# Retention and a squared-ReLU feed-forward on one core: two groups of retention products for each chunk instead of three

## The chip, the core and the metric

The kernel runs on one core of a Trainium2 chip. A core has a matrix engine (TensorE, "PE" in the profile; its weight loads are listed as "PEld"), a vector engine (VectorE, "DVE"), a scalar engine (ScalarE, "ACT"), a general engine (GpSimd, "POOL") and a queue that issues the transfers (SyncE, "SP"). Each engine works through its own list of instructions, and engines wait for each other only where one needs what another has made. The metric is the time of the program on the device, in microseconds (us).

## The reference

Two blocks stand one behind the other. The first is retention, an attention with a fixed decay in place of a softmax, for 8 batches of 8 heads, 576 positions and head size 64. The second is a feed-forward over all 4608 tokens, 512 to 2048 to 512, with a squared ReLU between.

```python
scores = scale * np.matmul(q, k.transpose(0, 1, 3, 2))
Dmat = np.where(rel >= 0, gamma[:, None, None] ** rel[None, :, :], 0.0)
ret = scores * Dmat[None, :, :, :]
attn_out = np.matmul(ret, v)
x = attn_out.transpose(0, 2, 1, 3).reshape(B * S, H * D)
h = np.maximum(x @ w_in, 0.0)
out = h * h @ w_out
```

`rel` is the distance between query and key, `gamma` differs by head. Since the decay is a power of the distance, it can be split into a factor for the query and one for the key, and what lies far back can be kept as one running 64x64 matrix per head.

## The kernel before

**Retention.** Each batch of 576 positions is cut into chunks of 128; the fifth chunk of a batch has only 64. There are 40 chunks, 8 of them short. A chunk is worked on in halves of 64 positions, and a head has size 64, so nearly all retention products are 64x64 products in a quarter of the TensorE array. For each chunk there are five pieces of TensorE work:

- `turn(i)` transposes k and q of the chunk (L364) into `t_ps`. ScalarE copies k to SBUF (`kT`, L370), and VectorE copies q out and multiplies it by the decay of the query (`qT`, L372). Both read the same banks, so the second waits for the first.
- `scores(i)` multiplies kT and qT of the same half (L385) into `sc_ps`, which takes the same PSUM buffer as `t_ps`. VectorE masks the result (`ret`, L388), and GpSimd multiplies v by the decay of the key (L390).
- `retain_a(i)` is the second half: scores times v within the half (L402) into `x_ps`, and the products of k and v of the first half (L405), which are added to the running matrix `u_ps`. ScalarE then copies the running matrix to SBUF (`u_sb`, L411).
- `retain_b(i)` is "q'U": the turned q times the running matrix, for both halves (L437), added into `x_ps`.
- `retain_c(i)` is the first half: scores times v (L402) and the running matrix again (L405), then its copy (L411), and the chunk's finished columns are copied from `x_ps` into `xT` (L463), where the feed-forward reads them.

The matmuls are float32; in the profile most of them stand as two records each, the transposes as one.

**A copy that orders things.** q'U and the first half add into the same columns of `x_ps`, from different rows of the array. Where other work lies between them, they are far enough apart. Where nothing lies between (the first four chunks and the last two), L447 makes a small copy on ScalarE: it reads one column of `x_ps` for each pair of heads, after q'U, and writes to a place in `u_sb` that is filled anew later. The first half waits for this copy.

**Feed-forward.** Tokens are taken in 9 blocks of 512. From the second block on, the first product (x times w_in) is not made directly: a 2x2 scheme with 7 products in place of 8 is used (`PRODUCTS`), so a block has 4 groups of 7 steps. One step, `ffn_in`, is four 128x128 by 128x256 products (eight records, L559), and each leaves work for VectorE (sums and squares, L566 to L586) or ScalarE and GpSimd (L569, L575, L576). The first block uses direct products (`first_in`, L525, 16 steps), while the weights are converted from 64-bit to 32-bit floats on VectorE and ScalarE: `convert(n)` runs the next n parts of that (L202 to L218). The second weights are converted in parts of a later list, one part behind each step. The results of the first product go to DRAM. When all retention is done, what remains of the first product follows, and then the second product runs as a stage of its own (`inner`, L748), again with 7 products, in two levels.

**The order.** The order on every engine is that of the program text: it is written out by hand in the loop of L647. Each pass mixes the retention of two neighbouring chunks with steps of the feed-forward. `ffn(i)` (L629) sets how many steps: it adds `cs / 3 * rate` to what is owed and takes steps until less than one is owed. The rate differs by stretch of tokens (L633 to L638). `retain_c` forces further steps at a block's end, so that buffers of `xT` come free (L459). Behind the fifth pass, a pass consists of three groups of retention products, with a call of `ffn` behind each: second half; q'U and scores of the next chunk; the chunk after that turned, and first half.

Of the kernel before, what the change touches and what calls it, by code (L numbers as in the profile page):

```python
# [16 lines left out]
CH = C // 2  # L17
# [23 lines left out]
def kernel(  # L41
# [33 lines left out]
    nc = tc.nc  # L75
# [16 lines left out]
    N_CH = len(chunks)  # L92
# [34 lines left out]
    def load(i):  # L127
        b, ci, c0, cs = chunks[i]
        got = {}
        for name, src, pool in (("k", k, ld4), ("q", q, ld3), ("v", v, ld4)):  # L130
            t = got[name] = pool.tile([128, H, D], F32, tag=name, name=f"{name}_ld")
            at = src[b, :, c0:c0 + cs, :].rearrange("h s d -> s h d")
            if name == "v":
                nc.sync.dma_start(t[:cs], at)
            else:

                nc.sync.dma_start(t[:cs, 0:H // 2, :], at[:, 0:H // 2, :])
                for e in range(2):
                    nc.sync.dma_start(t[:cs, H // 2 + e::2, :], at[:, H // 2 + 1 - e::2, :])
            if i < NCH and name == "q":  # L140
                nc.sync.dma_start(dq[:, :, c0:c0 + cs], decay_q[:, :, c0:c0 + cs])
        if i == 0:
            nc.sync.dma_start(dv, decay_v)
        loaded[i] = [got["q"], got["k"], got["v"]]
# [155 lines left out]
    def convert(count):  # L300
        for _ in range(count):
            f = next(w_in_steps, None)
            f and f()
# [20 lines left out]
    u_sb = [only.tile([128, HP, D], F32, name=f"u_sb{j}") for j in range(3)]  # L324
# [3 lines left out]
    N_EARLY = TOK // C  # L328
# [12 lines left out]
    def rows(half, n=64):  # L341
        return slice(64 * half, 64 * half + n)
# [4 lines left out]
    xp = [None]  # L347
    clean = set()

    def clears(half, bank):  # L350

        new = (half, bank) not in clean
        clean.add((half, bank))
        return new

    def turn(i):

        cs, c0 = chunks[i][3], chunks[i][2]
        n_h = cs // CH
        p = ps_t.tile([128, 2, 512], F32, tag="t", name="t_ps").rearrange("p h (j d t) -> p h j d t", j=2, d=HP)  # L360
        for j in (1, 0):
            for hp in range(HP):
                for h in range(n_h):
                    nc.tensor.transpose(p[:, h, j, hp, :], loaded[i][j][rows(h), 2 * hp:2 * hp + 2, :],  # L364
                                        ident[rows(h), rows(h)])
        for j, name in ((1, "kT"), (0, "qT")):
            t = st[i][name] = work2.tile([128, HP, C], F32, tag=name, name=name) if j == 0 else work.tile([128, HP, C], F32, tag=name, name=name)
            to = t[:, :, :cs].rearrange("p d (h t) -> p h d t", h=n_h)
            if j:
                nc.scalar.copy(to, p[:, :n_h, j, :, :])  # L370
            else:
                nc.vector.tensor_tensor(to, p[:, :n_h, j, :, :], dq[:, :, c0:c0 + cs].rearrange("p d (h t) -> p h d t", h=n_h),  # L372
                                        op=ALU.mult)
# [22 lines left out]
    def within(i, h):  # L396

        s = st[i]
        b_, ci, c0, cs = chunks[i]
        own, grow = [], []  # L400
        for hp, e, b in HEADS:
            own.append(lambda hp=hp, e=e, b=b: nc.tensor.matmul(  # L402
                x_at(hp, b, h), lhsT=s["vs"][rows(h), 2 * hp + b, :], rhs=s["ret"][rows(h), e, hp, :],
                start=clears(b, hp // 2), stop=False, skip_group_check=True))
            grow.append(lambda hp=hp, e=e, b=b: nc.tensor.matmul(  # L405
                u_ps[0][rows(e), hp, :], lhsT=loaded[i][1][rows(1 - h), 2 * hp + e, :], rhs=s["vs"][rows(1 - h), 2 * hp + b, :],
                start=(ci == 0 and h == 1 and hp == 0), stop=(hp == HP - 1), skip_group_check=True))
        return own, grow

    def grown(i, h):  # L410
        nc.scalar.copy(u_sb[(2 * chunks[i][1] + h + 1) % 3], u_ps[0])  # L411

    def retain_a(i):

        b_, ci, c0, cs = chunks[i]
        xp[0] = ps_x.tile([128, 2, 256], F32, tag="x", name="x_ps", padded_shape=[128, 2, 512])
        clean.clear()
        if ci == 0:
            u_ps[0] = ps_u.tile([128, HP, D], F32, tag="u", name="u_ps")
        if cs < C:  # L420
            return
        own, grow = within(i, 1)
        for j in range(0, len(own), 2):
            for f in own[j:j + 2] + grow[j:j + 2]:
                f()
        grown(i, 0)

    def retain_b(i):

        s = st[i]  # L430
        b_, ci, c0, cs = chunks[i]
        for h in reversed(range(cs // CH)):
            if 2 * ci + h == 0:
                continue
            u = u_sb[(2 * ci + h) % 3]
            for hp, e, b in HEADS[0:2] + HEADS[4:6] + HEADS[2:4] + HEADS[6:8]:
                nc.tensor.matmul(x_at(hp, b, h), lhsT=u[rows(e), hp, :], rhs=s["qT"][rows(e), hp, CH * h:CH * h + CH],  # L437
                                 start=clears(b, hp // 2), stop=False, skip_group_check=True)

    def retain_c(i):  # L440

        b_, ci, c0, cs = chunks[i]
        own, grow = within(i, 0)
        more = ci + 1 < NCH
        if i < N_EARLY or i >= N_CH - 2:

            nc.scalar.copy(u_sb[(2 * ci + (cs // CH)) % 3][:, 0:2, 0:1], xp[0][:, :, cs - CH:cs - CH + 1])  # L447
        for j in range(0, len(own), 2):
            for f in own[j:j + 2] + (grow[j:j + 2] if more else []):
                f()  # L450
        if more:
            grown(i, 1)
        tok = b_ * S + c0
        at = tok
        p = xp[0][:, :, 0:256].rearrange("p a (g t) -> p a g t", g=2)
        while at < tok + cs:
            n = at // TOK

            while steps and steps[0][0] <= (n - 2 if n > 4 else n - 3):  # L459
                step()  # L460
                owed[0] -= 1
            end = min(tok + cs, (n + 1) * TOK)
            nc.scalar.copy(xT[n][:, :, at - n * TOK:end - n * TOK].rearrange("p (a g) t -> p a g t", a=2),  # L463
                           p[:, :, :, at - tok:end - tok])
            at = end
            if n_next[0] < N_BLK and (n_next[0] + 1) * TOK <= at:
                steps.extend(block_steps(n_next[0]))
                n_next[0] += 1
        st[i] = loaded[i] = None
# [139 lines left out]
    owed = [0.0]  # L609
# [3 lines left out]
    def block_steps(n):  # L613
        if n == 0:
            return [(0, first_in, j) for j in range(N_W1)]
        return [(n, ffn_in, n, mp, j) for mp in range(N_MP) for j in range(NP)]

    def step():
        n, f, *args = steps.pop(0)
        f(*args)  # L620
# [8 lines left out]
    def ffn(i):  # L629

        b, ci, c0, cs = chunks[max(0, min(i, N_CH - 1))]
        tok = b * S + c0
        if tok < TOK + R_0:  # L633
            rate = (N_W1 - 2) / R_0 if tok >= TOK else 0
        elif tok < 5 * TOK:
            rate = (3 * N_MP * NP - LAG) / (4 * TOK - TOK - R_0 + TOK)
        else:
            rate = N_MP * NP / TOK  # L638
        owed[0] += cs / 3 * rate
        while steps and owed[0] >= 1:  # L640
            owed[0] -= 1
            if steps[0][0] == 0:
                convert(4)
            step()

    turn(0)
    for i in range(N_CH + 1):  # L647
        if i <= N_EARLY:

            if i >= 1:  # L650
                retain_a(i - 1)
                retain_b(i - 1)
                convert(2 if i >= 2 else 0)
                retain_c(i - 1)
            scores(i)
            convert(1 if i >= 2 else 0)
            if i == N_EARLY:
                step()
            turn(i + 1)
            convert((0, 2, 2, 2, 3)[i])  # L660
            if i == N_EARLY:
                step()
        else:
            retain_a(i - 1)
            convert(1)
            ffn(i - 1)
            retain_b(i - 1)
            if i < N_CH:
                scores(i)
            convert(1)  # L670
            ffn(i - 1)
            if i + 1 < N_CH:
                turn(i + 1)
            retain_c(i - 1)
            convert(1)
            ffn(i - 1)
        if i + 3 < N_CH:
            load(i + 3)
        if i < N_EARLY:
            fetch_raw(1 if i < 2 else 2)  # L680
# [183 lines left out]
```

## Time and profile before

| | |
|---|---|
| time, median of 3 runs | 1021.84 us (1021.08 to 1021.9) |
| span of the profiled execution | 1016.3 us |
| TensorE busy | 978.9 us (96%) |
| VectorE busy | 750.3 us (74%) |
| ScalarE busy | 184.6 us (18%) |
| mean of a record: step of the feed-forward (L559), retention product (L402) | 384 ns, 234 ns |

The stages, from the busy time of the engines in stretches of the span:

| us from the start | what runs | TensorE busy | VectorE busy | ScalarE busy | DMA share |
|---|---|---|---|---|---|
| 0 to 43.5 | first chunks, no feed-forward | 24.55 | 13.22 | 14.17 | 0.87 |
| 43.5 to 127 | retention and first block | 78.89 | 69.62 | 35.35 | 0.73 |
| 127 to 320 | retention and steps of 7 products | 192.72 | 149.12 | 41.00 | 0.67 |
| 320 to 556 | the same, with the second weights | 230.44 | 193.63 | 55.32 | 0.70 |
| 556 to 634 | the rest of the first product | 74.95 | 54.90 | 6.92 | 0.92 |
| 634 to 1016 | second product | 377.36 | 269.77 | 31.82 | 0.50 |

A line of the timeline has the start, the time up to the end of the last record, engine, line, operation, what is written and read, the size of the array that is used (128*128 or a part), the shape, and the number of records; in brackets stands how long the engine sat idle before, and for whom. Records of TensorE overlap, so the time from one start to the next says what work costs, not the length of one record. A line of the waits has who waited for whom, the total, how often, and the longest.

### The profile page before, as it was taken

The page shows a single profiled execution, that of the slowest core. Times are in us where ns is not written, and L with a number is a line of the kernel's source. Part 1 is how long each engine was busy: PE and PEld are TensorE (multiplying, and loading weights), DVE is VectorE, ACT ScalarE, POOL GpSimd, SP SyncE. Part 2 cuts the span into 40 slices and gives each one's busy share as a digit, 9 for nine tenths or more (in the row PEclk, how much of TensorE's full clock was granted, in tenths as well). Part 3 has the DMA queues.
Part 4 walks back from the last instruction along what each step waited for, and adds up shares of the span by engine and source line. Part 5 has one row for each costly group of instructions (what it writes and reads, how often), then busy time and mean ns, then how long its engine had stood idle before and what let it go on. Part 6 is the DMA issues. An engine that isn't in the chain of part 4 may idle for free.

```text
span 1016.3 us, 23980 instructions
## 1 busy us (share of the span) xinstructions
PE 978.9 (96%) x10376; PEld 860.9 (85%) x10376; DVE 750.3 (74%) x1398; ACT 184.6 (18%) x425; POOL 80.5 (8%) x82
## 2 busy tenths in 40 slices
PE   4799999999999999999899998999999999999998
PEld 3555488888888788888788888999999999999997
DVE  1489888657788797888976776767677676767765
ACT  2345321111213212222221010000000000000000
POOL 1110011101101112010110010000000000000000
PEclk9999999999999999999999999999999999999999
DMA  8877777647677769579446998473653636455351
GB/s 189 228 183 229 188 229 192 183 115 208 197 226 245 204 232 293 173 249 272 153 167 251 360 413 331 193 265 140 244 191 143 249 129 245 165 210 210 122 208 42
DMA packets 180232, 215.08 MB, mean 212 GB/s; under 512 B 118432, under 2 KB 128672, under 8 KB 171168
## 3 DMA queue, kind: packets, MB, share of 16 engines
q1 hardware_dynamic: 180128, 213.57, 63.8%
q8 instruction: 81, 1.33, 0.5%
q14 instruction: 23, 0.19, 0.1%
HBM read 125.19 MB, written 88.34 MB: 210 GB/s over the span
## 4 chain that ended last, share of the span: by engine, by line
PE 89%; DVE 5%; DMA 3%; ACT 1%; SPq 1%; issue 1%; DVEq 0%; ACTq 0%
PE o_b L748 16%; PE h_b L559 16%; PE o_c L748 11%; PE o_a L748 11%; PE h_a L559 10%; PE h_c L559 10%; PE h_ps L525 6%; PE x_ps L402 4%; PE t_ps L364 2%; PE x_ps L437 2%; PE sc_ps L385 2%; DMA a<-g_dram 1%; DMA w<-in_moe_w_in_dram 1%; DVE room L566 1%; PE u_ps L405 1%
## 5 line engine op out<-in xcount | busy, mean ns | idle before, releaser
L559 PE MATMUL h_b<-room,w 128*128 128x256 f32 x736 | 177.5, 384 | 1.2 <-DVE room L578 1.2
L559 PEld LDWEIGHTS h_b<-room,w 128*128 128x128 f32 x736 | 136.9, 190 | 21.1 <-DVE room L578 1.6
L748 PE MATMUL o_b<-w,room 128*128 128x128 f32 x1168 | 144.5, 275 | 0.2 <-DVE room L720 0.2
L748 PEld LDWEIGHTS o_b<-w,room 128*128 128x128 f32 x1168 | 137.2, 192 | 0.5 <-DVE room L720 0.4
L748 PE MATMUL o_c<-w,room 128*128 128x128 f32 x1008 | 123.0, 275 | 0.0
L748 PEld LDWEIGHTS o_c<-w,room 128*128 128x128 f32 x1008 | 117.7, 192 | 0.0
L559 PE MATMUL h_c<-room,w 128*128 128x256 f32 x480 | 115.8, 384 | 0.0
L559 PE MATMUL h_a<-room,w 128*128 128x256 f32 x448 | 107.5, 383 | 0.0
L559 PEld LDWEIGHTS h_c<-room,w 128*128 128x128 f32 x480 | 89.3, 190 | 12.8
L559 PEld LDWEIGHTS h_a<-room,w 128*128 128x128 f32 x448 | 83.8, 190 | 12.3 <-issue 0.5
L748 PE MATMUL o_a<-w,a 128*128 128x128 f32 x688 | 85.9, 275 | 2.8 <-DMA a<-g_dram 2.8
L748 PEld LDWEIGHTS o_a<-w,a 128*128 128x128 f32 x688 | 81.3, 192 | 3.0 <-issue 3.0
L566 DVE SCALAR_TENSOR_TENSOR room<-room 128x512 f32<-128x512 f32 x96 | 71.0, 739 | 3.3
L576 POOL TENSOR_TENSOR room<-room 128x512 f32<-128x512 f32 x32 | 35.9, 1122 | 433.6 <-ACT room L575 394.4
L759 ACT COPY r<-o_a 128x128 f32<-128x128 f32 x54 | 14.3, 265 | 276.9 <-PE o_a L748 236.2
L402 PEld LDWEIGHTS x_ps<-ret,v_ld 64*64 64x64 f32 x1152 | 42.4, 143 | 23.4 <-issue 13.9
L402 PE MATMUL x_ps<-ret,v_ld 64*64 64x64 f32 x1152 | 52.6, 234 | 9.2 <-ACT u_sb L447 5.3
L525 PE MATMUL h_ps<-room,w 128*128 128x512 f32 x128 | 59.7, 610 | 0.2 <-ACT room L463 0.2
L578 DVE TENSOR_TENSOR room<-h_b,room 128x512 f32<-128x512 f32 x32 | 22.1, 690 | 42.9 <-PE h_b L559 42.9
L372 DVE TENSOR_TENSOR qT<-t_ps,dq 128x512 f32<-128x512 f32 (+1 forms) x40 | 25.4, 634 | 36.1 <-ACT kT L370 25.8
L390 POOL TENSOR_TENSOR v_ld<-v_ld,dv 128x512 f32<-128x512 f32 (+1 forms) x40 | 44.4, 1110 | 95.5 <-DMA v_ld<-in_v_dram 74.4
L755 DVE TENSOR_TENSOR small<-o_b,small 128x128 f32<-128x128 f32 x63 | 18.4, 291 | 40.2 <-PE o_b L748 40.2
(92 smaller groups left out, 1355.5 us busy)
## 6 DMA issues: line engine op xcount, KB each, us to landing
g_dram<-room SPq DMA_DIRECT2D x36, 1792.0 KB, 7.4
a<-g_dram SPq DMA_DIRECT2D x43, 1024.0 KB, 6.3
room<-g_dram SPq DMA_DIRECT2D x20, 1024.0 KB, 6.0
w<-w_dram SPq DMA_DIRECT2D x7, 1792.0 KB, 12.3
out_dram<-room SPq DMA_DIRECT2D x18, 512.0 KB, 3.3
v_ld<-in_v_dram SPq DMA_DIRECT2D x32, 256.0 KB, 4.0
w<-in_moe_w_in_dram SPq DMA_DIRECT2D x16, 512.0 KB, 5.1
w<-in_moe_w_out_dram SPq DMA_DIRECT2D x16, 512.0 KB, 3.9
```

The source lines that it names most:

```text
L364: nc.tensor.transpose(p[:, h, j, hp, :], loaded[i][j][rows(h), 2 * hp:2 * hp + 2, :], ident[rows(h), rows(h)])
L372: nc.vector.tensor_tensor(to, p[:, :n_h, j, :, :], dq[:, :, c0:c0 + cs].rearrange("p d (h t) -> p h d t", h=n_h), op=ALU.mult)
L385: nc.tensor.matmul(sc[rows(h), e, hp, :], lhsT=kT[rows(e), hp, t], rhs=qT[rows(e), hp, t], start=True, stop=True, skip_group_check=True)
L390: nc.gpsimd.tensor_tensor(vs[:cs], vs[:cs], dv[:cs, :, ci:ci + 1].to_broadcast([cs, H, D]), op=ALU.mult)
L402: own.append(lambda hp=hp, e=e, b=b: nc.tensor.matmul(x_at(hp, b, h), lhsT=s["vs"][rows(h), 2 * hp + b, :], rhs=s["ret"][rows(h), e, hp, : ...
L437: nc.tensor.matmul(x_at(hp, b, h), lhsT=u[rows(e), hp, :], rhs=s["qT"][rows(e), hp, CH * h:CH * h + CH], start=clears(b, hp // 2), stop=Fa ...
L525: nc.tensor.matmul(p.rearrange("p h t -> p (h t)"), lhsT=w[:, c, :], rhs=xT[0][:, c, :], start=(c == 0), stop=(c == N_DM - 1))
L559: nc.tensor.matmul(p[:, mm, :], lhsT=w[:, c, :], rhs=xs[n][right][:, c, :], start=(j in OPENS and mm == 0 and c == 0), stop=(j in CLOSES a ...
L566: nc.vector.scalar_tensor_tensor(t, t, 0.0, t, op0=ALU.max, op1=ALU.mult)
L576: nc.gpsimd.tensor_tensor(g["A11"], g["A11"], g["A11"], op=ALU.mult)
L578: nc.vector.tensor_tensor(g["A22"], p, p15, op=ALU.add)
L748: nc.tensor.matmul(p, lhsT=s["lefts"][left][:, m, :], rhs=w_out[j][:, m, WO_SLOT[right], :], start=(i in OPENS and m == 0), stop=(i in CLO ...
```

## The change

The pass behind the fifth is written anew. The next chunk is turned directly behind the second half, one pass later than before, and the first half follows scores directly. So two groups remain: second half and the next chunk turned; q'U, scores and first half. Each is followed by one call of `ffn`, which now adds half of a chunk's share instead of a third. Since q'U and the first half have moved together, the ordering copy is made for every chunk, directly behind q'U. The aim is fewer changes of TensorE between small and full products.

```diff
@@ retain_b / retain_c
+        nc.scalar.copy(u_sb[(2 * ci + (cs // CH)) % 3][:, 0:2, 0:1], xp[0][:, :, cs - CH:cs - CH + 1])
+
     def retain_c(i):
...
-        if i < N_EARLY or i >= N_CH - 2:
-
-            nc.scalar.copy(u_sb[(2 * ci + (cs // CH)) % 3][:, 0:2, 0:1], xp[0][:, :, cs - CH:cs - CH + 1])
@@ ffn
-        owed[0] += cs / 3 * rate
+        owed[0] += cs / 2 * rate
@@ the loop
-            turn(i + 1)
+            if i < N_EARLY:
+                turn(i + 1)
             convert((0, 2, 2, 2, 3)[i])
...
         else:
             retain_a(i - 1)
-            convert(1)
+            if i < N_CH:
+                turn(i)
+            convert(2)
             ffn(i - 1)
             retain_b(i - 1)
             if i < N_CH:
                 scores(i)
-            convert(1)
-            ffn(i - 1)
-            if i + 1 < N_CH:
-                turn(i + 1)
             retain_c(i - 1)
             convert(1)
             ffn(i - 1)
```

## The prediction

> **What bounds the kernel now.** I read the share of busy time first, then the stages, then TensorE's timeline over one chunk, and last its waits up to 560 us, where the retention ends.
>
> ```profile
> PE 978.9 (96%) x10376; PEld 860.9 (85%) x10376; DVE 750.3 (74%) x1398; ACT 184.6 (18%) x425; POOL 80.5 (8%) x82
> ...
> PE 89%; DVE 5%; DMA 3%; ACT 1%; SPq 1%; issue 1%; DVEq 0%; ACTq 0%
> ```
>
> TensorE is busy 96% of the span and makes up 89% of the chain that ended last. In 127 to 320 us, inside the stage that changes, it is busy 192.72 of 193 us while VectorE has 149.12 and ScalarE 41.00. So in this stage the time is the sum of TensorE's issue slots, and only what shortens that sum, or a wait in it, counts. One chunk in that stretch:
>
> ```profile
> 279.56 1.99 PE L559 MATMUL h_b<-room,w 128*128 128x256 f32 x8
> 281.39 1.89 PE L559 MATMUL h_a<-room,w 128*128 128x256 f32 x8
> 283.21 0.69 PE L437 MATMUL x_ps<-qT,u_sb 64*64 64x64 f32 x32
> 283.73 0.65 PE L385 MATMUL sc_ps<-qT,kT 64*64 64x64 f32 x32
> 284.30 1.99 PE L559 MATMUL h_b<-room,w 128*128 128x256 f32 x8
> 286.13 1.89 PE L559 MATMUL h_c<-room,w 128*128 128x256 f32 x8
> 287.86 1.89 PE L559 MATMUL h_a<-room,w 128*128 128x256 f32 x8
> 289.68 0.46 PE L364 MATMUL t_ps<-ident,k_ld 64*128 64x64 f32 x8
> ```
>
> The first column is the start. Between two feed-forward steps a step takes 1.73 us (286.13 to 287.86). The step after a retention group takes 1.83 (284.30 to 286.13), the one before a group 1.82. So each entry and exit costs a tenth of a microsecond outside the group. From 279.56 to 284.30 is 4.74 us; less two steps of 1.728 the group of q'U and scores, 64 records, costs 1.284. The same sum where q'U has 16 records instead of 32 (262.40 to 268.64, three steps) gives 1.056, so a record costs (1.284 - 1.056) / 16 = 0.014, and 64 of them 0.91: the group has a fixed cost of **0.37 us**. The second half alone (273.56 to 279.56, three steps, 32 records) costs 0.816, again 0.36 above its records. Now the waits before the retention's products:
>
> ```profile
> PE x_ps L437 <- ACT u_sb L411: 5.9, 8, 2.3
> ...
> PE x_ps L402 <- ACT u_sb L447: 5.3, 5, 1.7
> PE t_ps L364 <- DVE ret L388: 4.9, 7, 0.9
> ...
> PE sc_ps L385 <- DVE qT L372: 2.0, 1, 2.0
> PE x_ps L402 <- ACT w L463: 1.6, 2, 1.1
> ```
>
> The columns are total, times, longest. The line to keep in mind is the second: it is the copy that the change now makes for every chunk, and today five of its six copies make TensorE wait.
>
> **What the Trainium skill says.** "TensorEngine Tiling (Array Packing)", Key Properties: changing the tiling mode drains TensorE, changing the tile does not. The trace agrees with 0.36 us for a visit, and with q'U and scores sharing one fixed cost. "PSUM — Partial Sum Buffer", PSUM bank collisions: two engines may not touch one bank and quadrant at once, and different row tiles must not write one bank together. That is why the copy of L447 is there: q'U and the first half reach the same bank from different rows. It is also why q's eviction (L372) comes after k's (L370): 25.8 us of VectorE's idle time end on it. "TensorE: Matmul & The Clock Gate", Architectural detail: ScalarE's queue is strictly first in, first out. So the copy waits for all that was queued ahead:
>
> ```profile
> 22.79 1.13 PE L437 MATMUL x_ps<-qT,u_sb 64*64 64x64 f32 x32 [2.30 <-ACT u_sb L411]
> ...
> 23.85 0.72 ACT L204 ACTIVATE w<-w,exp_bias 128x512 uint32<-128x512 uint32 x1 [1.11 <-DVE w L202]
> 24.48 0.64 ACT L209 ACTIVATE w<-w 128x512 f32<-128x512 uint32 x1
> 25.02 0.14 ACT L447 COPY u_sb<-x_ps 128x2 f32<-128x2 f32 x1
> ...
> 25.21 0.37 PE L402 MATMUL x_ps<-ret,v_ld 64*64 64x64 f32 x2 [1.29 <-ACT u_sb L447]
> ```
>
> The products end at 23.92, the copy takes 0.14, but it stands behind two weight conversions.
>
> **The change, part by part.** *Fewer visits.* I followed the loops with the rates of ffn and counted runs of retention work between feed-forward steps: 100 before, 69 after, since some calls of ffn give no step. That is 31 visits less. The upper price is 0.36, as q'U and scores show. The lower is the entry and exit alone, 0.10 + 0.09 = 0.19: turned chunk plus first half lasts 1.27 from its first start to the next step, and this is what the parts take singly (0.64 for a turned chunk at 47.71 us, 0.63 for a half), so a change between those two shapes eats the rest. That joint exists before and after (turn beside a half); the new joint is scores to first half, both 64*64. I take 0.35: **-10.8 us** (-5.9 to -11.2).
>
> *Waits that go.* (1) For the first four chunks the copy now comes ahead of the conversions on ScalarE. The waits there are 0.28, 1.29, 1.71 and 1.23; 0.28 is what the copy costs when nothing is queued ahead. Three excesses make 3.4; part will be lost to loads and to VectorE's conversions there, so -2.5 (0 to -3.4). The 0.74 near the end becomes 0.3: -0.4. (2) q'U waited for the running product's copy (L411) in four later chunks where ffn gave no step between, 2.1 in all; the turned chunk, 0.64, now lies between: -2.1. (3) Transposes waited for the masked scores (L388) in four later places, 2.3; they now follow a product that needs the same scores: -2.3. (4) The second half waited for L463 three times, 2.7; the loop now leaves one chunk without a step there: -1.9. Sum **-9.2**.
>
> *Waits that come.* (5) Where ffn gives no step between turned chunk and scores (three chunks: the fifth, and two after a forced run of steps), scores wait for k's copy, then q's product. Transposes start, 0.82 us later k's copy starts, 0.59, then 0.69, with hand-overs 2.2 us in all (272.29 to 274.5 by these durations); transposes and q'U fill 0.92 to 1.15. Three waits of 1.05 to 1.3: **+3.4**. (6) The first half waits for the copy in every chunk. With q'U of 32 records starting at 0, its results end at 0.69, the copy 0.06 later and takes 0.15, release 0.06: 0.96. Scores hold TensorE until 1.09, so it is hidden by a tenth. A ScalarE operation of the step before (L569, 0.59) starts 0.10 after q'U starts and ends at 0.69, so it hides too. Exposed are the seven chunks with half the scores (scores end at 0.81: 0.15 each), one chunk in which a weight's L204 waits for VectorE ahead of the copy (about 2 us), and scattered ones in the first stage: **+3.5** (1 to 10). (7) The copy's release comes so late that the weight load of the first half can't run ahead, up to 0.1 in 33 chunks: I take **+1.0**. (8) Runs of four steps in place of two or three let VectorE, busy 82% in 320 to 556 us, fall further behind; its one wait today is 1.2 us: **+0.5**.
>
> At nothing: the moved turn needs q and k later than before, loads are issued at the same place, and the two buffers of qT suffice, so the queue of loads is not changed; 3 calls at a third or 2 at a half give the same number of steps; after 634 us no instruction changes, and what precedes it is set off by TensorE's steps, so the gain is carried through.
>
> Sum: -10.8 - 9.2 + 3.4 + 3.5 + 1.0 + 0.5 = -11.6. From 1021.8 that is **1010.2 us**.
>
> **Rivals.** *The joint saves only entry and exit* (0.19): for it speaks the turned chunk beside a half, which saved no more; against it q'U beside scores, of the same shape as the new joint. Then 5.9 in place of 10.8: 1015.1. *The copy takes the place of the switch.* If ScalarE is late in most chunks, the first half waits some 0.7 us each time, as near the end (0.74), in 35 chunks: 24.5 in place of 3.5, which gives 1031.2, slower than before. For it: five of six copies are waited for today. Against: scores, 0.57 us, now lie between, and ScalarE is busy only a fifth of that stage. *The gain is lost elsewhere*: in 556 to 634 us DMA is 92% busy and TensorE meets a transfer at its end (2.8 us); if VectorE in the middle or these transfers set the pace, only a few microseconds of removed waits remain, 1020.5. Against: today TensorE idles 3 us of those 78, and the transfers start from its steps.
>
> **How the numbers follow.** Forecast 0.66, joint worth less 0.17, copy exposed 0.09, gain lost 0.08. The range goes from 1005.5 (early waits and visits in full, no exposed copy: -16) to 1018: the joint rival with the upper end of (6) would be 1021.6, of which I leave out the last part. Faster by over 0.2%: 0.84 (the first two, and a mild form of the third); within 0.2%: 0.08; slower: 0.08.
>
> **What would show it.** In the trace after: q'U, scores and first half in one run that costs 1.74 us over its steps, second half and turned chunk 1.47; two entries per chunk; L402 waiting for L447 about 3 to 5 us in all; scores waiting for L372 three more times; the L463, L388 and L411 waits after 43 us nearly gone. Wrong if L402 waits for L447 in most chunks, if the joint of scores and first half shows a gap of 0.1 or more, or if the stretch from 556 us to the end grows.

## The result, and the profile after

The changed kernel takes **1028.76 us** (median of 4 runs, 1027.09 to 1031.37) where the kernel before takes 1021.87 in the same comparison: a ratio of 1.007, 95% interval 1.0047 to 1.0093. The forecast was 1010.2, and faster. In the profiled executions the span grows from 1016.3 to 1027.4 us. That of the kernel before was a quick one: it took 1018.01 us at a mean granted TensorE clock of 0.999, where most of its executions on record took 1019 to 1024 at 0.996 or 0.997, so some 4 of the 11.1 us between the two traces are the clock of that one execution and not the change.

Lines move by one or a few in the changed kernel: the ordering copy is L440 (L447 before), a step of 7 products L558 (L559), a step of the first block L524 (L525), the chunk's last copy L462 (L463). First busy time and the chain that ended last, from the page of the changed kernel:

```profile
PE 981.0 (95%) x10376; PEld 869.2 (85%) x10376; DVE 750.7 (73%) x1398; ACT 190.7 (19%) x459; POOL 80.9 (8%) x82
...
PE 83%; DVE 11%; ACT 2%; DMA 2%; SPq 1%; issue 1%; DVEq 0%; ACTq 0%
```

VectorE does the same 1398 instructions in the same time, yet its part of the chain has gone from 5% to 11%, and TensorE's from 89% to 83%. So TensorE now waits for VectorE's results. Where, the waits of TensorE say (total, times, longest):

```profile
PE x_ps L402 <- ACT u_sb L440: 11.2, 13, 2.7
PE sc_ps L385 <- DVE qT L372: 8.0, 4, 3.1
PE x_ps L402 <- DVE ret L388: 6.0, 2, 5.5
...
PE x_ps L437 <- ACT u_sb L411: 3.8, 4, 2.3
...
PE t_ps L364 <- DVE ret L388: 2.5, 3, 0.9
```

The last two are down, as forecast (5.9 and 4.9 before). The first three are up from 5.3, 2.0 and nothing. The longest of all stands in the first block. TensorE's timeline there:

```profile
104.77 0.46 PE L437 MATMUL x_ps<-qT,u_sb 64*64 64x64 f32 x16
105.05 0.65 PE L385 MATMUL sc_ps<-qT,kT 64*64 64x64 f32 x32
105.67 0.68 PE L402 MATMUL x_ps<-ret,v_ld 64*64 64x64 f32 x16
111.88 0.37 PE L402 MATMUL x_ps<-ret,v_ld 64*64 64x64 f32 x2 [5.52 <-DVE ret L388]
...
113.99 5.22 PE L524 MATMUL h_ps<-room,w 128*128 128x512 f32 x8
119.14 0.46 PE L437 MATMUL x_ps<-qT,u_sb 64*64 64x64 f32 x16
```

Scores are made at 105.05, the first half of the chunk before at 105.67, and the next piece of work is the second half, which needs the masked scores. Half the share of a short chunk gave no step there. VectorE's timeline in the same stretch shows where the masked scores are:

```profile
106.93 1.54 DVE L532 TENSOR_TENSOR room<-room 128x512 f32<-128x512 f32 x1
108.51 0.69 DVE L500 TENSOR_TENSOR room<-room 128x512 f32<-128x512 f32 x1
...
110.45 0.69 DVE L486 TENSOR_TENSOR room<-room 128x512 f32<-128x512 f32 x1
111.05 0.68 DVE L388 TENSOR_TENSOR ret<-sc_ps,msk 128x512 f32<-128x512 f32 x1
```

VectorE works without a pause through what earlier steps left (squares, sums, conversions), and comes to L388 5.4 us after the scores are complete. In the kernel before, a step, a turned chunk and the first half lay between scores and their use, and 5.5 us passed anyway. But VectorE was not late for these scores there. They were complete at 106.25, and its timeline has:

```profile
106.33 0.69 DVE L388 TENSOR_TENSOR ret<-sc_ps,msk 128x512 f32<-128x512 f32 x1
```

The step that starts this square and these sums came behind the scores in the kernel before, and comes ahead of them now (ScalarE takes its result at 109.92 there, and at 104.88 in the changed kernel). What it puts ahead of L388 fills 4.1 of the 5.4 us. So at this place the new order made most of the lag; it did not only uncover one.

One more thing is to be read from the step at 113.99: it takes 5.15 us up to the next start, where such a step otherwise takes 3.63. TensorE's granted clock fell there. The three lines are the stretch from 100 to 120 us of the kernel before, of the changed one, and of the filled kernel told of below; the clock is the third figure from the right:

```profile
100.00:120.00 20.00, 19.43 (x242) 10.17 (x240) 19.21 (x31) 7.38 (x15) 2.47 (x2) 1.00 0.75 190
```

```profile
100.00:120.00 20.00, 14.48 (x198) 8.20 (x196) 13.40 (x20) 4.57 (x11) 3.12 (x2) 0.83 0.55 140
```

```profile
100.00:120.00 20.00, 18.96 (x240) 10.12 (x240) 15.75 (x23) 5.29 (x13) 2.71 (x2) 1.00 0.61 157
```

The clock is 0.83 on the mean there, 0.76 in 258 to 265 us and 0.83 in 380 to 390 and 480 to 490, each time behind a wait of 2.1 us or more; it is 1.00 in all four stretches in the trace of the kernel before. Inside these stretches the changed kernel has the clock at 0.50 for 6.8 us from 110.3, and for 3.4 us from 260.5, 383.3 and 485.7. The last of these begins 1.7 us after the wait has ended:

```profile
485.73:489.14 3.41, 3.41 (x10) 2.67 (x9) 1.70 (x3) 0.00 (x0) 0.00 (x0) 0.50 0.93 181
```

"TensorE: Matmul & The Clock Gate" of the Trainium skill, What's actually happening, says that TensorE runs at half rate after an idle window of about 3.4 us. The halving agrees (a step of 1.83 us took 3.44 at 260.57); here waits of 2.1 to 3.1 us were enough at times, and in a kernel below 1.6 and 1.8 us. Around most of these waits TensorE has only 64x64 products; whether these count less for the clock, no run shows.

**Where the time went.** The same ScalarE operation behind the same step (L530, L569 and L575 of the kernel before) can be paired in the two traces. The changed kernel is ahead by 3.2 us at 48 us and by 5.0 at 110. Then it loses 8.2 us up to 116, 5.6 at 258, 5.3 at 378, and 3.8 at 481. A smaller loss, 2.2 at 321, goes with a wait of 1.5 us for the copy. Between these places it gains on the whole, by 0.3 us for a chunk where no wait stands. At 560 us it is 9.7 behind and stays there to the end of that stage.

### The profile page after: what moved, and what is told of

Read it like the earlier page. It is cut to its first block, busy times and chain, and to the rows that moved or that the text cites. A ratio compares the mean times of both kernels' runs of the same rounds, so it can differ in the third digit from the quotient of the medians.

```text
span 1027.4 us, 24002 instructions
## 1 busy us (share of the span) xinstructions
PE 981.0 (95%) x10376; PEld 869.2 (85%) x10376; DVE 750.7 (73%) x1398; ACT 190.7 (19%) x459; POOL 80.9 (8%) x82
## 4 chain that ended last, share of the span: by engine, by line
PE 83%; DVE 11%; ACT 2%; DMA 2%; SPq 1%; issue 1%; DVEq 0%; ACTq 0%
PE o_b L746 16%; PE h_b L558 15%; PE o_a L746 11%; PE o_c L746 11%; PE h_a L558 10%; PE h_c L558 9%; PE x_ps L402 3%; PE h_ps L524 3%; PE t_ps L364 2%; DVE room L565 2%; PE x_ps L437 1%; PE sc_ps L385 1%; DMA a<-g_dram 1%; DVE w L218 1%; DVE w L215 1%
## 5 line engine op out<-in xcount | busy, mean ns | idle before, releaser
L558 PE MATMUL h_b<-room,w 128*128 128x256 f32 x736 | 176.8, 383 | 0.0
L558 PEld LDWEIGHTS h_b<-room,w 128*128 128x128 f32 x736 | 138.4, 190 | 19.6
L558 PE MATMUL h_c<-room,w 128*128 128x256 f32 x480 | 115.2, 383 | 0.0
L558 PE MATMUL h_a<-room,w 128*128 128x256 f32 x448 | 110.4, 390 | 0.0
L558 PEld LDWEIGHTS h_c<-room,w 128*128 128x128 f32 x480 | 91.4, 192 | 13.0
L558 PEld LDWEIGHTS h_a<-room,w 128*128 128x128 f32 x448 | 84.9, 193 | 12.6
L402 PE MATMUL x_ps<-ret,v_ld 64*64 64x64 f32 x1152 | 53.2, 236 | 18.7 <-ACT u_sb L440 11.2
L575 POOL TENSOR_TENSOR room<-room 128x512 f32<-128x512 f32 x32 | 35.2, 1099 | 448.4 <-ACT room L574 409.7
L524 PE MATMUL h_ps<-room,w 128*128 128x512 f32 x128 | 61.0, 625 | 0.2 <-ACT room L462 0.2
```

The source lines that it names most:

```text
L402: own.append(lambda hp=hp, e=e, b=b: nc.tensor.matmul(x_at(hp, b, h), lhsT=s["vs"][rows(h), 2 * hp + b, :], rhs=s["ret"][rows(h), e, hp, : ...
L524: nc.tensor.matmul(p.rearrange("p h t -> p (h t)"), lhsT=w[:, c, :], rhs=xT[0][:, c, :], start=(c == 0), stop=(c == N_DM - 1))
L558: nc.tensor.matmul(p[:, mm, :], lhsT=w[:, c, :], rhs=xs[n][right][:, c, :], start=(j in OPENS and mm == 0 and c == 0), stop=(j in CLOSES a ...
L575: nc.gpsimd.tensor_tensor(g["A11"], g["A11"], g["A11"], op=ALU.mult)
```

## Experiments

Each ratio is to the kernel before, run on the same chip; not all experiments ran on one chip, so ratios are compared, not times. The theory behind the first four: VectorE is several microseconds behind TensorE, and the change put consumers where less TensorE work hides that. The rivals: the ordering copy is dear in itself, or the new joint is; or VectorE sets the pace, and nothing but less work for it helps.

**The early copies alone.** The kernel before, with the copy of the first four chunks put behind q'U.

```diff
 def retain_b(i):
...
+        if i < N_EARLY:
+            nc.scalar.copy(u_sb[...][:, 0:2, 0:1], xp[0][...])
 def retain_c(i):
-        if i < N_EARLY or i >= N_CH - 2:
+        if i >= N_CH - 2:
```

> The kernel before with one part of the change alone: for the first four chunks the ordering copy stands directly behind q'U, ahead of the conversions. Theory (all of this part is on TensorE's path): the waits of L402 for the copy there fall from 4.5 to 1.1 us, and the time falls by 3.4 to 3.7 to about 1018.3. Rival (conversions of the first weights set the pace later on): 1021 to 1022.

1017.77 us, ratio 0.9964 (0.9952 to 0.9975). The waits of the first four fell from 4.5 to 1.1, and the kernel stays 2.6 us ahead from 59 us up to 501. By the medians this part of the change is worth 3.5 us, and all of it holds. (The profiled execution, its slowest, has 1.0 us left at 509: its clock is at 0.50 in 503.4 to 506.8, behind waits of 1.2, 1.3 and 0.5 us, where that of the kernel before is at 1.00 behind the same waits.)

**Conversion parts behind the copy.**

```diff
-            convert(2)
+            hold[0] = 1
             ffn(i - 1)
+            hold[0] = 0
             retain_b(i - 1)
+            convert(2)
+            for f in held:
+                f and f()
+            held.clear()
...
-            f and f()
+            held.append(f) if hold[0] else f and f()
```

> The changed kernel with one difference: the parts of the weight conversion that the steps between turned chunk and q'U would start, and the two parts called there, are issued behind the ordering copy instead of ahead of it. Theory (VectorE is some 3 us behind TensorE, and a conversion's L204 on ScalarE waits for it with the copy queued behind): the waits of L402 for the copy fall from 11.2 us to about 3, the slow clock after 258 and 481 us goes, time about 1019. Rival (the copy costs its wait wherever it stands, or the joint of scores and first half is dear in itself): no change, 1028 to 1029. Rival (VectorE sets the pace of the middle stage): the waits move elsewhere, 1025 to 1028.

1033.95 us, ratio 1.0127 (1.0111 to 1.0143): slower than the changed kernel, against all three. The waits for the copy did fall, from 11.2 to 2.0. A new one came, by the waits of this kernel and by its VectorE timeline:

```profile
PE h_b L558 <- DVE room L577: 8.8, 4, 5.3
```

```profile
145.04 0.43 DVE L202 TENSOR_SCALAR w<-w 128x512 uint32<-128x512 uint32 x1 [7.37 <-DMA w<-in_moe_w_out_dram]
```

The held parts include those that start the loads of the second weights. The load came late, VectorE stood 7.4 us at L202 with all of the steps' work queued behind, and a step waited 5.35 us. So this run mixes two causes.

**A step in each call of ffn.**

```diff
-        while steps and owed[0] >= 1:
+        least = 1
+        while steps and (owed[0] >= 1 or least):
+            least = 0
             owed[0] -= 1
```

> The changed kernel with one difference: a call of ffn takes at least one step if any is there, so that scores never follow the turned chunk, nor the second half the first, with no step between; what is owed is kept, so the number of steps in all is the same. Theory (TensorE meets VectorE's late q product and late masked scores exactly there, and an idle time of some 2 us and more brings a stretch at half clock): waits of scores for L372 fall from 8.0 to about 2 us, of L402 for L388 from 6.0 to under 1, the slow stretches at 107 and 384 us go, time about 1014.5. Rival (VectorE sets the pace): the same waits come back at other places, 1025 or more. Rival (the ordering copy is the whole loss): under 2 us gained.

1024.74 us, ratio 1.0026 (1.0015 to 1.0036): some 4 us better than the change, not 14. The waits at 112, 383 and 517 us fell from 5.52, 3.07 and 1.77 to 1.77, 1.09 and 1.43, and the slow stretch behind the second went. Behind the first it became half as long, 3.4 us:

```profile
117.14:120.54 3.40, 3.40 (x20) 1.74 (x17) 3.40 (x7) 0.85 (x2) 0.00 (x0) 0.50 0.50 186
```

In the first block the first half now waited for the copy four times, 0.8 to 1.7 us each, and behind one of these waits, of 1.56 us, the clock was at 0.50 too (55.7 to 59.1). What was won at the masked scores there came back at the copy: by 135 us this kernel is 2.7 us behind the kernel before, the changed one 2.5. In the first block the rival was right.

**Both.** The two edits above together, with the late load.

> Both differences of the two kernels before this one. Theory: the two gains add, since they are at different places: about 1005, 17 us below the kernel before, which is what 31 fewer visits at 0.31 to 0.35 us, the early copies (3.7) and the removed waits should give. Rival (VectorE sets the pace): not below 1020. Rival (fewer visits save little): about 1012.

1023.05 us, ratio 1.0018 (1.0009 to 1.0027). The late load is in it (a wait of 5.76 us at 145), so it does not decide between theory and rival.

**The hold without the load.** Held are only parts of the fourth block and later, and `convert(2)` stays where it was.

```diff
+            held.append(f) if hold[0] and n >= 3 else f and f()
```

> The changed kernel; only the parts of the second weights' conversion that steps of the fourth block and later start between turned chunk and q'U are issued behind the ordering copy. What the first such attempt moved besides, the loads of the second weights and two parts of the first weights' conversion, stays where the changed kernel has it. Theory (copy queued behind a conversion that waits for a late VectorE, and slow clock after the longer ones): the attempt lost its gain to the late load alone (a step waited 5.35 us at 146 us behind a conversion that waited for its data); now the waits at 260, 276, 326 and 484 us go, 7.2 us and some 2.5 us of slow clock, less 3 to 4 us of steps waiting for the parts bunched behind the copy: about 1023. Rival (what is not waited for at the copy is waited for elsewhere, in full): 1028.

1023.85 us, ratio 1.0027 (1.0011 to 1.0044), as the theory had it. In its trace the waits for the copy fall from 11.2 to 5.2 us, and the four that were to go are gone. The copy is not dear in itself: the same 40 copies are made, and what they stand behind in ScalarE's queue decides. One such place in the changed kernel, TensorE's timeline and then ScalarE's:

```profile
256.63 0.65 PE L385 MATMUL sc_ps<-qT,kT 64*64 64x64 f32 x32
259.93 0.71 PE L402 MATMUL x_ps<-ret,v_ld 64*64 64x64 f32 x16 [2.65 <-ACT u_sb L440]
260.57 3.60 PE L558 MATMUL h_a<-room,w 128*128 128x256 f32 x8
264.01 1.89 PE L558 MATMUL h_b<-room,w 128*128 128x256 f32 x8
```

```profile
259.02 0.72 ACT L204 ACTIVATE w<-w,exp_bias 128x512 uint32<-128x512 uint32 x1 [5.62 <-DVE w L202]
259.64 0.14 ACT L440 COPY u_sb<-x_ps 128x2 f32<-128x2 f32 x1
```

ScalarE was idle for 5.6 us, waiting for VectorE at L204, with a copy of 0.14 us behind it. The step at 260.57 shows the slow clock again.

**Hold and a step.** The last two edits together.

> The kernel before this one, and at least one step in each call of ffn. Theory: the gain of at least one step (4 us, measured) and that of the later conversions (6) are at different places and add: about 1019. Rival (VectorE sets the pace): 1023 or more.

1017.26 us, ratio 0.9959 (0.9944 to 0.9975). The gains add; the 2 us beyond their sum are within the intervals.

**Three groups in the first block.** The same, but up to chunk 12 the loop of the kernel before runs (three groups, a third of the share).

```diff
+    TWO = 12
...
+        elif i < TWO:
+            retain_a(i - 1)
+            convert(1)
+            ffn(i - 1, 3)
+            retain_b(i - 1)
+            scores(i)
+            convert(1)
+            ffn(i - 1, 3)
+            turn(i + 1)
+            retain_c(i - 1)
+            convert(1)
+            ffn(i - 1, 3)
...
```

> The kernel before this one, with three groups as in the kernel before up to the chunk where the steps of 7 products begin (chunk 12), and two groups behind it. Theory (in the first block VectorE has no time to spare, and half a chunk's share leaves no step between scores and the second half that need VectorE's result): up to 127 us it runs as the kernel before with early copies, 2.6 to 3.5 us ahead, in place of 1 to 3 behind, about 1014, and faster than the kernel before. Rival (VectorE sets the pace in the later stages too): 1020 or more.

**1013.02 us**, ratio 0.9918 (0.9896 to 0.9941): faster than both kernels. The waits of its TensorE (the copy is L442 there, qT L373, the masked scores L389):

```profile
PE sc_ps L386 <- DVE qT L373: 4.7, 4, 1.5
...
PE x_ps L403 <- ACT u_sb L442: 2.1, 6, 0.6
...
PE x_ps L403 <- DVE ret L389: 1.2, 1, 1.2
```

The early copies alone gave 0.9964. What lies beyond, 0.46% or 4.7 us, comes with two groups in the later stages, held parts and a step in each call together. So two groups there do pay, once VectorE's results are not asked for too soon, and this is against the rival that VectorE sets the pace throughout. The trace has 22 entries into retention fewer than that of the kernel before, 6.8 us at the 0.31 us found below. Held parts with three groups all the way were not run.

**The first block alone.** The changed kernel with three groups up to chunk 12, and nothing else.

> The changed kernel with nothing moved, but three groups up to chunk 12 and two groups behind it. Theory: it differs from the changed kernel by the first block alone, 4.5 to 5.5 us (the wait of 5.5 us for masked scores and the slow clock after it, less the visits saved there): about 1024. Rival (the loss of the change is all behind 127 us): 1028 to 1029.

1023.37 us, ratio 1.0021 (1.0013 to 1.0029). By the ratios, about 5 us of the loss are in the first block.

**The clock.** Idle time filled with products that nobody reads.

```diff
+    def fill(count):
+        p = ps_f.tile(...)
+        for c in range(count):
+            nc.tensor.matmul(p, lhsT=ident, rhs=dq[:, 0, 0:512], start=(c == 0), stop=(c == count - 1))
...
+            if i == 28:
+                fill(3)
             scores(i)
             retain_c(i - 1)
+            if i == 10:
+                fill(5)
```

> The changed kernel with work added that nobody reads: five products of 128x128 by 128x512 between the first half of one chunk and the second half of the next where TensorE waited 5.5 us for masked scores, and three ahead of scores where it waited 3.1 us for q (about 0.9 us each, so they end before what is waited for). Theory (the slow steps behind these waits come from the clock, which falls when TensorE idles): the waits shrink to under 1 us without anything arriving sooner, the steps behind them take 3.6 and 1.7 us in place of 5.2 and 2.5, and the time falls by the slow stretches alone, 2.4 + 1.4 us, to about 1025. Rival (the steps are slow because they wait for operands or memory): no change or later, 1028.5 to 1030.

1025.80 us, ratio 1.0072 (1.0053 to 1.0092); the kernel before had a median of 1018.99 on that chip. By the paired operations the two filled places cost 3.7 us less, but the ratio shows nothing. So both kernels ran once more on one chip:

> The changed kernel once more, as the other half of a pair with the filled kernel on one chip. All theories: 0.6 to 0.8% over the kernel before.

> The filled kernel once more, beside the changed kernel on the same chip. Theory (the falling clock makes 3.7 us at the two filled places, as the trace of the first filled run shows): 3 to 4 us, 0.3 to 0.4%, under the changed kernel. Rival (the filling only shifts the slow stretches, or adds as much as it saves): within 1 us of it.

The changed kernel took 1031.56 us (ratio 1.0089, 1.0067 to 1.0111), the filled one **1025.66** (1.0043, 1.0027 to 1.0059): 5.9 us less by the medians, with more instructions. In the filled kernel's timeline:

```profile
106.13 4.56 PE L648 MATMUL fill_ps<-dq,ident 128*128 128x512 f32 x10
111.73 0.27 PE L402 MATMUL x_ps<-ret,v_ld 64*64 64x64 f32 x2 [1.04 <-DVE ret L388]
...
113.00 3.70 PE L524 MATMUL h_ps<-room,w 128*128 128x512 f32 x8
```

The second half starts at 111.73 as before (111.88); nothing came sooner. But it and the step behind are done at 116.63, not at 119.14. The two traces are 6.9 us apart at 560 us. By the paired operations some 5 of these are at the two filled places, and 1.6 at 258 us, where nothing was filled: TensorE waits 2.65 us there in both, and the clock of 258 to 265 us is 0.76 in one and 1.00 in the other. So the clock also makes the time of the changed kernel uncertain.

**Further spreading.** To the kernel of 1013 us: held parts are made two to a step, and a call takes at least two steps.

> The kernel with three groups up to chunk 12, with two differences: the conversion parts held back are made two to a step in the steps that follow, not all behind the copy, and a call of ffn takes at least two steps behind chunk 12. Theory (what is left of VectorE's lateness is bunched parts and the two places with a single step between turned chunk and scores): the steps' waits for L579 (3.2 us) and of scores for q (2.8 us after the start) go: about 1009.5. Rival (it only moves): 1013.

1014.67 us, ratio 0.9956 (0.9938 to 0.9975): no gain over it. It is 8.5 us ahead of the kernel before at 443 us, and then scores wait 3.84 us for q at 445, and a slow step follows. Here the rival holds: the wait only moved.

**The price of a visit.** The kernel before with one more group for each chunk.

```diff
             retain_b(i - 1)
+            ffn(i - 1)
             scores(i)
...
-        owed[0] += cs / 3 * rate
+        owed[0] += cs / 4 * rate
```

> The kernel before with one more group for each chunk: a call of ffn stands between q'U and scores too, each call a quarter of the share. It makes 25 more runs of retention work between steps (119 in place of 94), and all distances between producer and consumer stay or grow. A visit at 0.31 to 0.36 us, the price used for the change: 7.8 to 9.0 us slower, about 1029.5. Rival (only entry and exit count, 0.19): 1026. Rival (visits cost nothing once waits are equal): 1021.

1041.81 us, ratio 1.0226 (1.0203 to 1.025): 23 us over the kernel before, where 7.8 to 9.0 were expected. From 418 to 465 us of the kernel before, where neither kernel waits, three visits more cost 1.05 us by the paired operations: 0.35 us each, as forecast. Over all 25 that makes some 9 us. The rest are largely waits again, and the clock behind the longest. Transposes waited 12.0 us for masked scores (4.9 before), 4.6 of it at 118 us in the first block, and the clock is at 0.50 from 117.5 to 124.2. "All distances stay or grow" was wrong in that expectation: with a quarter of the share no step stood between scores and transposes at times.

## Why the prediction was wrong

The mechanism it bet on is there, and the step that failed is the waits that come, items (5) to (8): it summed them to 8.4 us. The trace has 22.0 us of such waits after 43 us (5.9 for q, 10.1 for the copy, 6.0 for masked scores), and the slow clock, put at nothing, behind the longest. From one chunk to the next, the changed kernel has:

```profile
285.03 1.99 PE L558 MATMUL h_b<-room,w 128*128 128x256 f32 x8
...
300.39 1.99 PE L558 MATMUL h_b<-room,w 128*128 128x256 f32 x8
```

- **Visits.** The price was nearly right (0.31 for 0.35), the count was not. The 15.36 us between these two starts hold seven steps (12.10) and 3.26 of retention (3.21 forecast). In the kernel before it was 15.67 us (279.56 to 295.23), with 3.57 of retention, so a chunk gains 0.31. But the traces have 93 entries before and 67 after: 26 less, not 31, because a chunk of 64 has no second half. That gives 8.1 us where 10.8 stood.
- **Waits that go.** Item (1) was put at 2.5 and brought 3.5 alone; (2) went as said, (4) brought 1.3 of its 1.9. Item (3) holds the error in one clause: transposes "now follow a product that needs the same scores". So they do, and that product had been moved next to the scores. The wait was not removed but handed to the second half, and in one place it was 5.5 us.
- **(5), scores behind the turned chunk.** The three places were right, and 3.4 us were forecast; they took 1.02 + 3.07 + 1.77 = 5.9. The chain was worked out with VectorE free at once. At 383 us it was still at squares, sums and conversions, and came to q 3.0 us after the transposes.
- **(6), the copy.** After 43 us it took 10.1 us and not 3.5; its range was 1 to 10. The margin of a tenth for a free ScalarE was right: most chunks show no wait. But only the last step ahead of q'U was looked at for a conversion. With VectorE up to 3 us behind, a conversion two steps back can still be in ScalarE's queue, and six places were exposed by 0.6 to 2.7 us.
- **(8), VectorE's backlog** was put at 0.5 and read from a busy share of 82%. A share does not tell how far behind an engine is. In the first block the trace of before had VectorE busy 19.2 of 20 us between 100 and 120, and the forecast never looked at this line. Nor did it ask what the new order puts ahead of the masked scores in VectorE's queue, which made most of the wait of 5.5 us.
- **The clock** was not in the forecast. Measured by longer steps, 2.4 us at 112, 1.6 at 260, 1.5 at 383 and 1.7 at 484 (two steps, 2.52 and 2.82 us): 7.2 us.

Put together: -8.1 visits, -3.5 early copies, waits after 43 us (without the end of the stage) from 10.4 to 23.4, +13.0, clock +7.2 make 8.6. The paired operations give 9.7 at 560 us, so about 1 us is not placed; the late weight loads of item (7), 1.0, may be a part. Another 1.4 us of the two profiled spans arise after that stage, where the program is the same. They are the clock again: at the start of the second product TensorE waits for a transfer in both, 2.81 us before and 2.64 in the changed kernel, and behind it the clock is 1.00 in the one trace (633.2 to 636.5) and 0.50 in the other (642.8 to 646.1): the first eight records take 0.97 us and 1.84. So the clock makes 8.6 us between the traces (7.2 and 1.4). Some 4 of them are the luck of the one execution of the kernel before, as said above; some 5 belong to the change.

The rival that came nearest, the copy exposed, named 0.7 us in most chunks and 1031. The time is near it, but the way was another: a few long waits, more than half of the time not at the copy. Leaving the copy out where scores lie between q'U and the first half was not tried, since nothing would then order the two.

## What to carry to other kernels

Work that lies between a producer and its consumer hides the lag of another engine, even when it was put there for another reason. Before groups are merged, read from the timeline how far behind the helping engine is at that place, not how busy it is. Then write down what the new order puts ahead of each result in that engine's queue, for a small new instruction too: a lag that the old timeline doesn't show can be made by the new order. Where a change brings idle stretches of the matrix engine of some 2 us, expect a slow clock behind part of them.

## What was not expected of the hardware

A wait of 1.6 to 3.1 us on TensorE was enough, in some executions, to halve its clock for 3.4 or 6.8 us: a step took 3.44 us in place of 1.83. The fall can come after the wait, 1.7 us behind its end at 485.7. Waits of 1.2, 1.3 and 0.5 us within 5 us were enough once (the early copies alone, at 503). Filling two such places with useless products made the program 5.9 us faster by the medians. Which of the waits do it differs between executions of one program: the filled kernel waits 2.65 us ahead of 259 us in both of its traces, and the clock of 258 to 265 us was 0.76 in the first and 1.00 in the second.
